# Early products of two output tiles moved into the last rounds of attention, with their loads and banks

## The chip, the cores and the metric

The kernel runs on one core of one Trainium2 chip. The metric is the device time of one execution in microseconds (us), from runs on the chip; the profile comes from one more execution of the same program, which has a time of its own.

## The reference, cut to what matters

x has 2048 rows of 576 numbers in float32. Four layers follow each other: attention, spectral filter, attention, spectral filter, each with a layer norm ahead and a residual behind. Both attention layers use the same weights.

```python
def _A_ref(x, wqkv, wo):                       # 32 heads of 18, window of 256
    q, k, v = split(x @ wqkv)                  # by heads
    scores = einsum("bhqd,bhkd->bhqk", q, k) * Dh ** -0.5
    p = softmax(where(0 <= i_q - i_k < 256, scores, -1e9))
    return heads_joined(einsum("bhqk,bhkd->bhqd", p, v)) @ wo
def _B_ref(x, w_r, w_i):
    return irfft2(rfft2(x) * (w_r + 1j * w_i))

x = x + _A_ref(_layernorm(x), A_wqkv, A_wo)
x = x + _B_ref(_layernorm(x), B_w_r, B_w_i)
x = x + _A_ref(_layernorm(x), A_wqkv, A_wo)
x = x + _B_ref(_layernorm(x), B_w_r, B_w_i)
```

## The kernel before, in words

Every factor of a product is split into a high and a low part of twelve bits of mantissa, so that a product of float32 is two or three products of the faster form (float32r); the parts are named h and l.

**Attention in rounds.** `layer_a` works on 8 groups of 4 heads (n), each with 16 blocks of 128 rows: NX = 128 units x. A loop over t runs from -10 to 129. Round t does the scores of unit t + 10 (LEAD = 10; matmul `S` on TensorE, row maximum with mask on VectorE, L879 to L882), the exponentials of unit t (matmul `E` on TensorE, `P` on ScalarE, masks on GpSimd, L907 to L914), and the product with v of unit t - 2 (`pv`, matmuls `U`, L927). A round handles heads in two pairs: `E` of a pair, `S` of the pair, and after the first pair `pv`. Up to round 102 the products of the q and k projection (`pj`) are spread behind the second pair. Round 117 is the last with scores; from round 118 on a round has only `E` and `U`. After every fourth unit ScalarE copies `U` out (`us`), and `norm` (L934 to L947) transposes it (`tpo`), divides, and stores the rows to DRAM: columns 0 to 447 of the attention's result to o_d, 448 to 575 to o7_d (both stores have line 947). `m_rows` (L884) turns the row maxima round (`tpm`) and sends them with two small DMAs into a row of the q stack.

**Banks.** PSUM has tiles of one bank. `bank` (L840) hands them out in the order of the list `banks`: three with tag S and two with tag E, and from round 103 also the two `pj` ones in front, which leave the list again at round OB + 5 = 125 (OB = NX - 8 = 120). U has a bank of its own. A bank is written again only when the engine that read it has finished.

**The output projection** is done in 16 output tiles u of 128 rows by the class `Out`. The work for a tile: load its rows from o_d (`load`, which also loads the rows of x), split the last 64 columns on GpSimd (`tail`), transpose on TensorE and split on ScalarE or VectorE (`turn`: four transposes, a copy for the high part, a subtraction for the low part), eleven steps of two products each with the first 448 columns (`early`, 22 matmuls `ops` of L578), the transposed last 128 columns (`turn_last`, `split_last`), three more steps (`late`), the sum with x on VectorE (L600), and the sums for the next layer norm (`sums`). `o7` holds the last 128 columns of all tiles; it is filled by the loads `last`, and its last 32 rows directly from the four transposes `tpz` (L1047). Before, ten loads of weights are issued in rounds 105 to 114, the loads of tiles 0 to 2 in 120 to 122, the constants of the next layer (`consts`, six DMAs) in 123, the turns of tiles 0 to 2 in 125 to 127, and all of `early` comes after the last round. DMAs named here are issued by SyncE (SP), in the order of the program: an issue that waits holds all behind it.

**After the rounds** the order is (L1042 to L1071): four steps of tile 0, the `tpz` transposes, the rest of tile 0, tile 1, `turn_last` and `split_last` of tiles 0 to 2, tile 2, `turn(3)`, then `late` of tiles 0, 1, 2 and `turn(4)`. The spectral layer then starts with the products of tile 3 in banks of a new pool.

The time of a round is set by the order in which the program lists work for each engine (no planner reorders it) and by the waits for banks and data.

## Time and profile before

| | us |
|---|---|
| median of 3 runs (1444.2 to 1447.67) | 1447.11 |
| the profiled execution's own time | 1444.81 |
| its span, first to last instruction | 1443.1 |
| TensorE matmul busy in it | 1358.7 (94%) |
| VectorE busy | 947.2 (66%) |
| ScalarE busy | 807.9 (56%) |
| GpSimd busy | 704.5 (49%) |

The mean granted TensorE clock is 0.982 of full speed. PE is the TensorE matmul, PEld its weight loads, DVE VectorE, ACT ScalarE, POOL GpSimd, SP SyncE. A row of the timeline gives the start, the time from the first start to the last end of a run of like instructions (which may overlap the next row's), the engine, the line of the kernel, the tile written and the tiles read, the shapes and the count; in brackets the idle time of the engine before it and what ended that. A product of float32 (`U`, transposes by `ident`) and one of float32r (`E`, `S`, `pj`, `ops`) are both shown as f32; a `U` product counts twice, so that x16 is one `pv`. Matmuls overlap: the distance from start to start is what a matmul costs PE, not its duration.

### The profile page before, as it was taken

Reading aid. Unit: us, or ns where it says so; the run is one execution under the profiler, and the core shown is the slowest. Engines: PE = TensorE matmul, PEld = TensorE weight load, DVE = VectorE, ACT = ScalarE, POOL = GpSimd, SP = SyncE. Lnnn points to the kernel's source line nnn. Section 1 sums busy time; section 2 is a strip of 40 time slices with the busy share of each in tenths; the row PEclk is TensorE's granted clock in tenths of the full one; section 3 lists DMA queues with packets and bytes.
Section 4 is the critical chain, followed back from the end, with each engine's and each line's share of the span. In section 5 each row is a group of like instructions: output and inputs, shape, how many; then the busy total and the mean of one; then the engine's idle time right before and its main releaser. Section 6 shows DMA issues by size and latency. Waiting matters only on the chain. (4 is left out here: it accounts for less than half of the span.)

```text
span 1443.1 us, 35833 instructions
## 1 busy us (share of the span) xinstructions
PE 1358.7 (94%) x12536; PEld 1060.7 (74%) x12536; DVE 947.2 (66%) x3055; ACT 807.9 (56%) x1905; POOL 704.5 (49%) x1203
## 2 busy tenths in 40 slices
PE   7999999999999999987979999999999999999878
PEld 7987666666665889846979876666666658898468
DVE  5348777887777465564543487777877865655645
ACT  5623676666768344425645236766677683443255
POOL 3346566666655343253612565655565553332535
PEclk9999999999999999998989999999999999999989
DMA  7866555545546657676675565555444565576766
GB/s 233 266 193 225 161 165 179 173 151 175 164 142 171 187 179 222 212 235 226 210 238 121 181 223 160 162 155 156 139 145 155 154 172 176 180 222 211 237 221 207
DMA packets 198661, 269.93 MB, mean 187 GB/s; under 512 B 87042, under 2 KB 109154, under 8 KB 197266
## 3 DMA queue, kind: packets, MB, share of 16 engines
q1 hardware_dynamic: 187872, 250.06, 56.1%
q10 hardware_dynamic: 10098, 14.35, 3.2%
q0 software_dynamic: 512, 3.23, 0.8%
q8 instruction: 101, 1.65, 0.5%
q14 instruction: 78, 0.64, 0.1%
HBM read 166.30 MB, written 103.79 MB: 187 GB/s over the span
## 5 line engine op out<-in xcount | busy, mean ns | idle before, releaser
L881 DVE CUSTOM_DVE_ANT_0 jk<-S,mask 128x384 bf16<-128x384 f32 (+2 forms) x1024 | 497.4, 529 | 89.8 <-PE S L879 85.2
L908 ACT ACTIVATE P<-E 128x384 f32<-128x384 f32 (+2 forms) x1024 | 422.5, 477 | 166.2 <-PE E L907 135.9
L910 POOL TENSOR_SCALAR_AFFINE_SELECT P<-P 128x512 f32<-128x512 f32 x256 | 162.4, 634 | 268.1 <-ACT P L908 250.0
L879 PE MATMUL S<-ks,qs 63*128 63x384 f32 (+2 forms) x1024 | 238.9, 364 | 4.3 <-DMA qs<-qk_d 1.0
L907 PE MATMUL E<-qs,ks 64*128 64x384 f32 (+2 forms) x1024 | 220.3, 393 | 2.9 <-DVE sg L823 0.7
L927 PE MATMUL U<-P,vq 128*19 128x128 f32 (+1 forms) x3840 | 202.8, 329 | 2.5 <-POOL P L913 2.0
L907 PEld LDWEIGHTS E<-qs,ks 64*128 64x128 f32 x1024 | 118.5, 183 | 78.1 <-issue 28.5
L879 PEld LDWEIGHTS S<-ks,qs 63*128 63x128 f32 x1024 | 132.7, 184 | 52.2 <-ACT P L908 23.5
L811 PE MATMUL pj<-xh,wqh 64*128 64x512 f32 (+1 forms) x640 | 165.5, 402 | 2.1 <-ACT vt L770 1.7
L927 PEld LDWEIGHTS U<-P,vq 128*19 128x19 f32 x3840 | 90.0, 98 | 95.2 <-issue 34.3
L913 POOL TENSOR_SCALAR_AFFINE_SELECT P<-P 128x512 f32<-128x512 f32 x224 | 142.1, 634 | 0.0
L811 PE MATMUL pj<-xl,wqh 64*128 64x512 f32 (+1 forms) x512 | 127.8, 392 | 0.0
L811 PE MATMUL pj<-xh,wql 64*128 64x512 f32 (+1 forms) x640 | 121.6, 392 | 0.0
L578 PE MATMUL ops<-oroom 128*128 128x288 f32 x784 | 115.2, 304 | 4.4 <-DVE oroom L561 3.0
L578 PEld LDWEIGHTS ops<-oroom 128*128 128x128 f32 x784 | 108.0, 194 | 6.2 <-DVE oroom L561 4.0
L811 PEld LDWEIGHTS pj<-xh,wqh 64*128 64x128 f32 (+1 forms) x640 | 87.7, 186 | 7.3 <-ACT vt L770 2.1
L186 POOL TENSOR_TENSOR eo<-xn 128x287 f32<-128x287 f32 x32 | 26.1, 816 | 126.6 <-ACT xn L184 121.6
L881 DVE DVE_READ_ACCUMULATOR2_ANT m<- 128x1 f32 x1024 | 85.3, 83 | 0.0
L811 PEld LDWEIGHTS pj<-xh,wql 64*128 64x128 f32 (+1 forms) x640 | 73.4, 186 | 7.3
L825 POOL TENSOR_TENSOR sg<-sg 128x512 fp32r<-128x512 f32 x56 | 72.2, 1289 | 4.7
L766 PE MATMUL vps<-wvh,xh 128*128 128x288 f32 x320 | 73.4, 312 | 0.9 <-ACT xh L500 0.9
L811 PEld LDWEIGHTS pj<-xl,wqh 64*128 64x128 f32 (+1 forms) x512 | 71.3, 186 | 3.7
(231 smaller groups left out, 2457.4 us busy)
## 6 DMA issues: line engine op xcount, KB each, us to landing
qk_d<-sg SPq DMA_DIRECT2D x56, 512.0 KB
qs<-qk_d SPq DMA_DIRECT2D x384, 72.0 KB
ks<-qk_d SPq DMA_DIRECT2D x384, 72.0 KB
v_d<-vt SPq DMA_DIRECT2D x32, 304.0 KB
vq<-v_d SPq DMA_DIRECT2D x16, 608.0 KB
wt<-in_w SPq DMA_DIRECT2D x16, 580.0 KB
x<-ofree SPq DMA_DIRECT2D x32, 288.0 KB
ofree<-x SPq DMA_DIRECT2D x16, 576.0 KB
```

The source lines that it names most:

```text
L186: P.tensor_add(eo[:, 0, 1:288], xn[:, 1:288], xn[:, 575:288:-1])
L578: self.nc.tensor.matmul(self.ps[u][n][:, 0:288], x, self.w[p][:, wk * D + n * 288:wk * D + n * 288 + 288], start=first and i == 0, stop=la ...
L766: T.matmul(ps[:, n, 0:288], xT(xk, c), w[:, wk, n * 288:(n + 1) * 288], start=i == 0, stop=i == len(ks) - 1)
L811: T.matmul(ps, w[r, wk], xT(xk, cs)[r], start=s == 0, stop=s == len(ks) - 1)
L825: (P if halves else V).tensor_sub(sg[:, 1], su, sg[:, 0].bitcast(F32))
L879: T.matmul(ps[:, 0:N], q[b:b + 63, pair, i * 128:i * 128 + 128], k[b:b + 63, pair, lo:hi], start=True, stop=True)
L881: V.tensor_tensor_reduce(out=jk[:, 0:N], in0=ps[:, 0:N], in1=mask[:, 384 - N:384], scale=1.0, scalar=-3e38, op0=ALU.add, op1=ALU.max, accu ...
L907: T.matmul(ps[:, 0:nq], k[b:b + 64, pair, j * 128:j * 128 + 128], q[b:b + 64, pair, j * 128:j * 128 + nq], start=True, stop=True)
L908: A.activation(p[:, hl_, 0:nq], ps[:, 0:nq], AF.Exp, scale=SC)
L910: P.affine_select(out=p[:, :, 0:128], in_=p[:, :, 0:128], pattern=[[0, 4], [1, 128]], compare_op=ALU.is_ge, fill=0.0, base=0, channel_mult ...
L913: P.affine_select(out=p[:, :, 256:384], in_=p[:, :, 256:384], pattern=[[0, 4], [-1, 128]], compare_op=ALU.is_gt, fill=0.0, base=0, channel ...
L927: T.matmul(U[32 * h:32 * h + 19, (q0 % 4) * 128:(q0 % 4) * 128 + 128 * (q1 - q0)], vts[n][:, j, h], pt[n, j][:, h, (q0 - j) * 128:(q1 - j) ...
```

## The change

Four products (two steps of two halves) a round of the early products of tiles 0 and 1 are put behind the second pair, in rounds 115 to 125 (`begun`); with them the main columns (0 to 383) of these two tiles are loaded in rounds 111 and 112 and turned in 114 and 118, and their 64-column tails and x follow in 116 and 117 and are turned together in 121 (`turn_tails`). The weights come in the order in which the steps want them, the constants one a round in 115 to 120, the last columns in three loads of 32 partitions. The two `pj` banks leave the rotation at round 113 and hold tile 0's sums; from round 118 two S banks hold tile 1's sums, and the exponentials go round in E, E and the third S bank (F), which later holds half of tile 2. After the rounds, tile 2's early products stand around `tpz` (four transposes each as `turn_z`), one half after the other, then `turn(3)`, `turn_last` and `split_last` of tiles 0 to 2, and the `late` steps as before.

```diff
@@ -506,7 +506,7 @@
     def __init__(self, nc, ident, eps, bp, ov, o7v, srcv, dstv, wo_d, dc_d, gc_d):
         self.__dict__.update(nc=nc, ident=ident, eps=eps, bp=bp, ov=ov, o7v=o7v, srcv=srcv, dstv=dstv, wo_d=wo_d, dc_d=dc_d, gc_d=gc_d)
-        self.ps = {}
+        self.ps, self.dcs = {}, []
     def room(self):
         self.rh = rh = self.bp.tile([128, 5 * S], F32R, tag="xh", name="oroom")
@@ -526,20 +526,24 @@
         self.o7 = f[:, 4736:6784].rearrange("p (n e) -> p n e", n=NT)
     def weights(self, k):
-        c = slice(k // 2 * D, k // 2 * D + D)
-        self.nc.sync.dma_start(self.w["hl"[k % 2]][:, c].bitcast(F32), self.wo_d[k % 2, :, c].bitcast(F32))
-
-    def consts(self):
-
-        self.dcs = []
-        for k, t in enumerate(("wraw", "wraw", "wqh", "wqh", "wql")):
-            d = self.bp.tile([128, 2, NF], F32R, tag=t, name=f"dc{k}", bufs=2)
+        p, b = ("h0", "h1", "h2", "l0", "l1", "l2", "h4", "l4", "h3", "l3")[k]
+        c = slice(int(b) * D, int(b) * D + D)
+        self.nc.sync.dma_start(self.w[p][:, c].bitcast(F32), self.wo_d["hl".index(p), :, c].bitcast(F32))
+
+    def consts(self, k):
+
+        if k < 5:
+            d = self.bp.tile([128, 2, NF], F32R, tag=("wraw", "wraw", "wqh", "wqh", "wql")[k], name=f"dc{k}", bufs=2)
             self.nc.sync.dma_start(d.bitcast(F32), self.dc_d[:, 2 * k:2 * k + 2].bitcast(F32))
             self.dcs.append(d)
-        self.nc.sync.dma_start(self.gc.rearrange("p a c -> p (a c)").bitcast(F32), self.gc_d.bitcast(F32))
-
-    def load(self, u):
-        self.nc.sync.dma_start(self.o[u % 3], self.ov[:, u])
+        else:
+            self.nc.sync.dma_start(self.gc.rearrange("p a c -> p (a c)").bitcast(F32), self.gc_d.bitcast(F32))
+
+    def load_main(self, u):
+        self.nc.sync.dma_start(self.o[u % 3][:, 0:384], self.ov[:, u, 0:384])
+
+    def load(self, u, c=slice(0, 448)):
+        self.nc.sync.dma_start(self.o[u % 3][:, c], self.ov[:, u, c])
         self.nc.sync.dma_start(self.x[u % 5], self.srcv[:, u])
     def last(self, r, c):
@@ -563,6 +567,20 @@
         if last is not None:
             self.split_last(u, last)
+    def turn_main(self, u, tp, copy):
+
+        T, o, oT = self.nc.tensor, self.o[u % 3], self.oT[u % 3]
+        for kt in range(3):
+            T.transpose(tp[:, kt * 128:kt * 128 + 128], o[:, kt * 128:kt * 128 + 128], self.ident)
+        copy(oT[:, 0:384], tp[:, 0:384])
+        self.nc.vector.tensor_sub(oT[:, 512:896], tp[:, 0:384], oT[:, 0:384].bitcast(F32))
+
+    def turn_tails(self, tp):
+        for u in range(2):
+            self.nc.tensor.transpose(tp[:, 128 * u:128 * u + 128], self.tl[u], self.ident)
+        self.nc.vector.tensor_copy(self.rh[:, 5760:7552].rearrange("p (k c) -> p k c", k=2)[:, :, 384:512],
+                                   tp[:, 0:256].rearrange("p (k c) -> p k c", k=2))
+
     def turn_last(self, u, tp):
         self.nc.tensor.transpose(tp, self.o7[:, u], self.ident)
@@ -572,13 +590,13 @@
         self.nc.scalar.copy(oL[:, 0:128], tp)
         self.nc.vector.tensor_sub(oL[:, 128:256], tp, oL[:, 0:128].bitcast(F32))
-    def steps(self, u, ks, first, last):
+    def steps(self, u, ks, first, last, halves=(0, 1)):
         for i, (x, p, wk) in enumerate(ks):
-            for n in range(2):
+            for n in halves:
                 self.nc.tensor.matmul(self.ps[u][n][:, 0:288], x, self.w[p][:, wk * D + n * 288:wk * D + n * 288 + 288],
                                       start=first and i == 0, stop=last and i == len(ks) - 1)
-    def early(self, u, ps, some=slice(0, 11)):
+    def early(self, u, ps, some=slice(0, 11), halves=(0, 1)):
         oT = self.oT[u % 3]
         c = lambda k: oT[:, 128 * k:128 * k + 128]
         if ps:
@@ -589,7 +607,7 @@
         for k in range(3):
             ks += [(c(k), "l", k)]
         ks += [(c(3), "h", 4), (c(3), "l", 4)]
-        self.steps(u, ks[some], some.start == 0, False)
+        self.steps(u, ks[some], some.start == 0, False, halves)
     def late(self, u):
         oL = self.oL[u % 3]
@@ -831,7 +849,7 @@
                             rest()
                 return [lambda s=s, k=k: mm(s, k) for s, k in enumerate(ks)]
-            banks, later, stores = ["S", "S", "E", "E", "S"], [], []
+            banks, later, stores, fixed = ["S", "S", "E", "E", "S"], [], [], []
             def store():
                 while stores:
@@ -842,6 +860,8 @@
                 tag = "S"
                 if t >= 0:
                     banks.append(tag := banks.pop(0))
+                if tag == "F":
+                    return fixed[0]
                 return pp.tile([128, 512], F32, name=name, tag=tag, bufs=3 if tag == "S" else 2)
             vts = {}
@@ -970,6 +990,8 @@
                     goal[t] = 84 + 14 * m - (-14 * (t + 1 - a) // (b - a))
             OB = NX - 8
+            begun = {OB - 5: [(0, 0, 2)], OB - 4: [(0, 2, 4)], OB - 3: [(0, 4, 6)], OB - 2: [(0, 6, 8)], OB - 1: [(0, 8, 9), (1, 0, 1)], OB: [(1, 1, 3)],
+                     OB + 1: [(1, 3, 5)], OB + 2: [(1, 5, 7)], OB + 3: [(0, 9, 11)], OB + 4: [(1, 7, 9)], OB + 5: [(1, 9, 11)]}
             out = Out(nc, ident, eps, bp, ov, o7v, srcv, dstv, wos, dc_d, gc_d)
             for t in range(-LEAD, NX + 2):
@@ -984,8 +1006,11 @@
                 if t == max(goal) + 1:
                     banks[:0] = ["pj", "pj"]
-                if t == OB + 5:
+                if t == OB - 7:
                     banks = [tag for tag in banks if tag != "pj"]
+                if t == NX - LEAD:
+                    first, fixed = [[pp.tile([128, 512], F32, tag="S", name=f"{k}_{n}", bufs=3) for n in range(z)] for k, z in (("ops1", 2), ("F", 1))]
+                    banks = ["E", "E", "F"]
                 want = goal.get(t, len(pj))
                 more, done = pj[done:want], want
                 for pair in range(2):
@@ -1003,6 +1028,9 @@
                         for f in more[:(len(more) + 1) // 2]:
                             f()
                         more = more[(len(more) + 1) // 2:]
+                    if pair == 1 and t in begun:
+                        for u, a, b in begun[t]:
+                            out.early(u, None, slice(a, b))
                 for f in more:
                     f()
                 if copy and t >= 32 and t % 4 == 0 and t < 32 + 16 * len(copy):
@@ -1021,44 +1049,65 @@
                     out.room()
                 if t in range(OB - 15, OB - 5):
                     out.weights(t - OB + 15)
-                if t - OB in (0, 1, 2):
-                    out.load(t - OB)
-                if t == OB + 3:
-                    out.consts()
+                if t - OB in (-9, -8):
+                    out.load_main(t - OB + 9)
+                if t - OB in (-4, -3):
+                    out.load(t - OB + 4, slice(384, 448))
+                if t == OB - 6:
+                    out.turn_main(0, pp.tile([128, 512], F32, tag="pj", name="tpm0", bufs=2), A.copy)
+                    out.ps[0] = [pp.tile([128, 512], F32, tag="pj", name=f"ops0_{n}", bufs=2) for n in range(2)]
+                if t == NX - LEAD:
+                    out.ps[1] = first
+                    out.turn_main(1, bank("tpm1"), V.tensor_copy)
+                if t - OB in (-1, 0):
+                    out.tail(t - OB + 1)
+                if t == OB + 1:
+                    out.turn_tails(bank("tpt"))
+                if t - OB in (0, 2, 3):
+                    out.load((2, 0, 3, 4)[t - OB])
+                if t in range(OB - 5, OB + 1):
+                    out.consts(t - OB + 5)
+                if t == OB + 1:
                     out.last(slice(96, 128), slice(0, 56))
-                if t == NX - 1:
-                    out.last(slice(0, 96), slice(0, 128))
-
-                if t - OB - 3 in (0, 1, 2, 4):
-                    out.tail(min(t - OB - 3, 3))
-                if t - OB - 5 in (0, 1, 2):
-                    u = t - OB - 5
-                    out.turn(u, pp.tile([128, 512], F32, tag="pj", name=f"tpa{u}", bufs=2), V)
-                    if u < 2:
-                        out.load(u + 3)
+                if t - OB in (1, 5, 7):
+                    c = (t - OB) // 3
+                    out.last(slice(32 * c, 32 * c + 32), slice(0, 128))
+
+                if t - OB in (4, 6):
+                    out.tail(2 + (t - OB) // 5)
+                if t == OB + 6:
+                    out.turn(2, bank("tpa2"), V)
                 if t == NX:
                     A.activation(wp.tile([128, 1], F32, name="se", bufs=1), eps, AF.Sqrt)
-            out.early(0, [pp.tile([128, 512], F32, tag="S", name=f"ops0_{n}", bufs=3) for n in range(2)], slice(0, 4))
-
-            for k in range(4):
-                tp = pp.tile([128, 512], F32, tag="E" if k in (1, 2) else "pj", name=f"tpz{k}", bufs=2)[0:32]
+            out.early(2, [fixed[0], None], slice(0, 8), (0,))
+
+            def turn_z(k, tp):
+
                 for a in range(4):
-                    T.transpose(tp[:, 128 * a:128 * a + 128], us[NQ - 1, 3][:, 4 * k + a:512:16], ident)
-                tv = tp.rearrange("p (a h e) -> p a h e", a=4, h=4)
+                    T.transpose(tp[0:32, 128 * a:128 * a + 128], us[NQ - 1, 3][:, 4 * k + a:512:16], ident)
+                tv = tp[0:32].rearrange("p (a h e) -> p a h e", a=4, h=4)
                 rc = wp.tile([128, 4, 4, 1], F32, tag="rc", name=f"rcz{k}", bufs=2)[0:32]
                 V.reciprocal(rc, tv[:, :, :, 18:19])
                 V.tensor_mul(out.o7[96:128, 4 * k:4 * k + 4, 56:128].rearrange("p a (h e) -> p a h e", e=18), tv[:, :, :, 0:18],
                              rc.to_broadcast([32, 4, 4, 18]))
-            out.early(0, None, slice(4, 11))
-            out.early(1, [pp.tile([128, 512], F32, tag=k, name=f"ops1_{k}", bufs=b) for k, b in (("S", 3), ("E", 2))])
-            tp = pp.tile([128, 512], F32, tag="pj", name="tpl", bufs=2)
+
+            def bank_e(name):
+                return pp.tile([128, 512], F32, tag="E", name=name, bufs=2)
+
+            turn_z(0, bank_e("tpz0"))
+            turn_z(1, bank_e("tpz1"))
+            turn_z(2, U)
+            out.early(2, None, slice(8, 11), (0,))
+            turn_z(3, bank_e("tpz3"))
+            out.ps[2][1] = bank_e("ops2_1")
+            out.early(2, None, slice(0, 11), (1,))
+            out.turn(3, U, A)
+            out.tail(4)
+            tp = bank_e("tpl")
             for f in (out.turn_last, out.split_last):
                 for u in range(3):
                     f(u, tp[:, 128 * u:128 * u + 128])
-            out.early(2, [pp.tile([128, 512], F32, tag=k, name=f"ops2_{k}", bufs=2) for k in ("E", "pj")])
-            out.turn(3, U, A)
-            out.tail(4)
             for u in range(3):
                 out.late(u)
                 if u == 0:
@@ -1068,7 +1117,7 @@
                 if u == 1:
                     out.turn_last(4, tp[:, 0:128])
                     out.split_last(4, tp[:, 0:128])
-            out.turn(4, pp.tile([128, 512], F32, tag="E", name="tpa4", bufs=2), A)
+            out.turn(4, pp.tile([128, 512], F32, tag="S", name="tpa4", bufs=3), A)
         spectral(dst, out.dcs, out.gc, ident, out.rh, out.rl, out)
         ctx2.close()
```

## Rows read from the trace of the kernel before

**Rows 1.** The page, busy time of each engine, share of the span and instructions:
```profile
PE 1358.7 (94%) x12536; PEld 1060.7 (74%) x12536; DVE 947.2 (66%) x3055; ACT 807.9 (56%) x1905; POOL 704.5 (49%) x1203
```
**Rows 2.** Chain of waits, 1100 to 1260 us: start, us, engine, tile, line, count:
```profile
1187.45 3.16 ACT P L908 x8
...
1193.71 6.23 DMA o_d<-o
1200.00 5.21 DMA ofree<-o_d
1205.26 0.55 PE tpl L567 x3
...
1214.94 5.50 PE ops L578 x28
1221.09 3.71 PE ops L578 x28
```
**Rows 3.** Timeline of PE, rounds with scores, one with and one without projection:
```profile
1123.39 0.85 PE L927 MATMUL U<-P,vq 128*19 128x256 f32 x16
...
1124.63 0.40 PE L811 MATMUL pj<-xl,wqh 64*128 64x512 f32 x2
...
1125.56 0.35 PE L907 MATMUL E<-qs,ks 64*128 64x384 f32 x2
...
1126.01 0.84 PE L927 MATMUL U<-P,vq 128*19 128x256 f32 x16
...
1170.88 0.85 PE L927 MATMUL U<-P,vq 128*19 128x256 f32 x16
...
1173.05 0.85 PE L927 MATMUL U<-P,vq 128*19 128x256 f32 x16
```
**Rows 4.** Busy time by stretch (us, then PE, PEld, DVE, ACT, POOL, PEclk, DMA, GB/s):
```profile
1164.00:1166.00 2.00, 1.99 (x25) 1.12 (x25) 2.00 (x9) 1.10 (x3) 0.64 (x1) 1.00 1.00 322
```
**Rows 5.** Timeline of PE, rounds without scores:
```profile
1176.46 0.35 PE L907 MATMUL E<-qs,ks 64*128 64x384 f32 x2
...
1184.08 0.85 PE L927 MATMUL U<-P,vq 128*19 128x256 f32 x16 [1.00 <-POOL P L913]
...
1185.22 0.66 PE L937 MATMUL tpo<-ident,us 128*128 128x128 f32 x4
...
1186.19 0.85 PE L927 MATMUL U<-P,vq 128*19 128x256 f32 x16
...
1187.51 0.85 PE L927 MATMUL U<-P,vq 128*19 128x256 f32 x16
...
1190.57 0.39 PE L907 MATMUL E<-qs,ks 64*128 64x256 f32 x2
```
**Rows 6.** Timeline of all engines, the tail after the last round:
```profile
1196.56 1.32 PE L578 MATMUL ops<-oroom 128*128 128x288 f32 x8
...
1197.72 1.91 PE L1047 MATMUL tpz<-ident,us 128*32 128x128 f32 x16
...
1199.39 2.09 PE L578 MATMUL ops<-oroom 128*128 128x288 f32 x14
...
1201.32 0.29 PE L578 MATMUL ops_S<-oroom 128*128 128x288 f32 x1
...
1206.47 0.27 ACT L572 CAST oroom<-tpl 128x128 fp32r<-128x128 f32 x1 [0.36 <-DVE oroom L573]
...
1209.20 0.59 ACT L560 CAST oroom<-U 128x512 fp32r<-128x512 f32 x1 [1.84 <-PE U L556]
...
1209.82 0.56 DVE L561 TENSOR_TENSOR oroom<-U,oroom 128x384 fp32r<-128x384 f32 x1 [2.14 <-ACT oroom L560]
...
1210.29 0.81 DVE L600 TENSOR_TENSOR ofree<-ofree,ops 128x288 f32<-128x288 f32 x2
```
**Rows 7.** Timeline of SP, the DMA issues of the constants:
```profile
1188.15 2.34 SPq L537 DMA_DIRECT2D dc<-dcr  x5
```
**Rows 8.** Busy time by stretch, columns as in rows 4, after the tail:
```profile
1215.50:1216.00 0.50, 0.50 (x4) 0.50 (x4) 0.00 (x0) 0.50 (x1) 0.00 (x0) 0.50 0.77 175
```

## The prediction

> **What bounds the kernel now.** I read the page first: TensorE (PE) is busy for 94% of the span [rows 1], so work that only changes its place gains nothing unless it lands where PE now stands idle. Then the chain of waits, around the end of the second attention: it runs through ScalarE's exponentials, a store to o_d of 6.23 us, the load that waits for it, 5.21 us, and only then to the transposes `tpl` at 1205.26 [rows 2]. There PE waits for a DMA, not for arithmetic. Third, PE's timeline, which shows three regimes. With scores, one group `U` stands 2.17 us after the last (1170.88 to 1173.05, [rows 3]), and in such a stretch VectorE is busy throughout [rows 4]: it sets the pace. Without scores (from the first `E` of round 118 at 1176.46) two groups `U` can stand 1.32 us apart, yet the eight rounds up to the first `E` of round 126 at 1190.57 take 14.11 us [rows 5]. ScalarE sets that pace: eight exponentials in 3.16 us are 1.58 us a round [rows 2], and PE, which runs ahead, waits 1.00 us once [rows 5]. In the tail, from 1196.56 (the first product `ops`) to 1210.29 (the first sum into x), 13.73 us, nearly all is PE [rows 6]. The first attention layer is the same program on another input, so every sum, made here for the second, counts twice.
>
> **What leaves the tail.** Of the 66 early products of tiles 0 to 2, 44 leave. The new tail on PE, from the first product on: 8 products 1.16 us (the distance to `tpz`); 12 of the 16 transposes `tpz`, which take 1.67 us to the next `ops`, 1.25; 3 products at 0.138 (14 in 1.93) 0.41; the other 4 transposes 0.42; 11 products 1.52; 4 transposes of `turn(3)`, 0.42 [rows 6]. That is 5.2 us. The copy of `turn(3)` starts 0.3 later and takes ScalarE 0.59, VectorE's subtraction behind it takes 0.56, and three splits follow at 0.63 us each (ScalarE's half 0.27, and 0.36 in which it waits for VectorE's half before) [rows 6]: 8.5 us to VectorE's first sum into x. Before, the 22 products of tile 2 lay beside the splits; now nothing does. So the tail is 13.73 - 8.5 = **5.2 us shorter** a layer. From that sum on the order stays, and the products at 1214.94 move with it.
>
> **Does the DMA chain let it?** The store of 6.23 us [rows 2] stands behind five loads of constants (297 kB each: 128 x 2 x 290 numbers) that SP issued from 1188.15 [rows 7]. They go to rounds 115 to 120, one a round, and the last load shrinks from 96 partitions to 32 (262 kB). Bounds for the store: 6.23, nothing gained; or its 147 kB at the pace of the 786 kB load, 151 kB/us, 1.0. The store has the smaller rows and some traffic still ahead, but not 1.5 MB; I take 2.5. The load at that pace is 1.7, which I double for its fixed part. The store is issued 2.85 us ahead of the tail, so the data land about 3.5 us into it; PE asks for them at 5.2. The wait for the DMA goes, and what is late next is the splits. On SP's queue six issues of constants, two of main columns and four of tails and x move ahead by 3 to 11 rounds, and tiles 2 to 4 by up to three; at 0.47 us each (2.34 for five, [rows 7]) that is at most 1.4 us in rounds of 1.6 and more. They pass the small DMAs that carry the row maxima, which are wanted four rounds after their issue; I cost them at nothing, and if that cover fails, exponentials wait for as long as the maxima are late. The order of the weights costs nothing either: ten issues before, ten after, in the same rounds.
>
> **What the rounds pay.** In each of eleven rounds (115 to 125) four products stand behind the second pair. Their own time is 4 x 0.138 = 0.55 us. To change from one kind of matmul to another costs PE too: the round with the four transposes `tpo` between its pairs of `E` is 2.11 us from `U` to `U` (1184.08 to 1186.19), the next, without, 1.32 [rows 5]; four transposes are 0.42, so the change costs 0.37. No row has `ops` between two `E`. I bound the overhead by 0 and 0.37 and take 0.2, since `U` to `ops` to `tpz` adds little (8 products in 1.16 us, [rows 6]): 0.75 us a round.
> In rounds 118 to 125 PE then needs 8 x 1.32 + 8 x 0.75 = 16.6 us and 1.7 for what else stands in them (`tpm`, two `tpo`, the main transposes of tile 1, two tails, at 0.42 or less each). That is 18.3 against 14.11: 4.15 more, less 0.3 because ScalarE isn't behind any more when round 126 begins, so **3.85** (2.6 without overhead, 5.2 with 0.37).
> In rounds 115 to 117 PE has slack: a round with products of the projection takes 2.62 us (1123.39 to 1126.01), 0.93 of which are these (1124.63 to 1125.56, [rows 3]), so PE's own need is 1.69 of the 2.17. Each round pays 0.75 - 0.48 = 0.27, three pay 0.8. Tile 0's split in round 114 gives VectorE, at its limit there, one more subtraction (0.56, [rows 6]), partly hidden, and from round 113 the two `pj` banks are out of the rotation: 0.5 for both. So **1.3** (0.4 to 2.0).
> The two together, 5.15, are what the tail gives back.
>
> **The sum.** -5.2 + 5.15 = -0.05 us a layer, nothing for two. The profiled execution took 1444.81 us (span 1443.1 and 1.7 around it), 2.3 less than the median of the runs; on it the sum gives 1444.7, on the median **1447.0**. By the ends of the terms, 2.2 gained or 2.0 lost a layer, 1442.7 to 1451.1.
> One more term can move. The 28 products after `turn(4)` take 5.50 us, the next 28 take 3.71 [rows 2]: the granted clock is 0.50 there, 1.2 GHz of the 2.4 [rows 8], after PE had worked in short pieces between waits. The new tail has such pieces too, so I leave the term at 0, with 0.9 us a layer either way.
>
> **The rivals.**
> *A: insertions cost their own time only.* Then the rounds pay 2.6 + 0.4 a layer, 2.2 is gained: 1442.7, and 1441.2 if the low clock shrinks too. For it: products of the projection between scores show no gap [rows 3]. Against it: 0.79 us for four transposes [rows 5].
> The Trainium skill's page "TensorE: Matmul & The Clock Gate" (Part 2, Step-by-step) says that PE pulls a weight load ahead of running matmuls when their row groups don't conflict or the spare weight buffer takes it. By that rule the overhead vanishes and A's time holds; the round with `tpo` speaks against it.
> *B: the smaller rotation of banks becomes the bound (slower).* From round 118 three banks (E, E, F) carry the exponentials where seven did, from 113 five. A bank comes back after its matmul, the exponential and two semaphores, about 1 us. When PE has been at `pv` or an insertion, the next `E` starts late, ScalarE starves, and `pv` waits for GpSimd's selects. For it: PE has waited for GpSimd's `P` already [rows 5]. Against it: with PE at 2.07 us a round ScalarE's 1.58 leaves 0.5 to return banks. At 0.37 us a round in the 16 rounds of both layers it adds 6 us: 1453. It decides from 0.27 us a round (4.3 us).
> *C: the DMA chain stays last.* If the store still takes 6.23 and the load 3.5, `tpl` starts 6.9 us into the tail, 1.7 late a layer: 1450.4. For it: this chain ends last now [rows 2]. Against it: 1.5 MB no longer stand ahead of it.
> That the early products don't run in the rounds at all I rule out: PE takes its work in the order of the program.
>
> **How the numbers follow.** Forecast 0.46, A 0.27, B 0.20, C 0.07. A measurement tells about 0.3% (4.3 us) from no change. Faster: most of A and the forecast's lower end, 0.25. Slower: B, part of C and the upper end, 0.26. No change: 0.49. The range goes from A with the better clock, 1441.2, to nearly B, 1452.8; the forecast's own is 1442.7 to 1451.1.
>
> **What would show it.** Right: groups `U` of rounds 118 to 125 near 2.05 us apart without waits of PE for ScalarE; rounds 118 to 126 near 18 us instead of 14.11; 8.5 us from tile 2's first `ops` to the first sum into x; no DMA before `tpl` in the chain, splits in its place. Wrong: rounds near 1.85 us (A), waits for `P` ahead of `E` (B), a piece `DMA o_d` in the chain (C). A tail less than 4 us shorter, or rounds that grow by under 3 us in all, would refute the sum.

## The result: slower by 0.43%

The changed kernel takes 1451.4 us (median of 7 runs, 1449.89 to 1454.67), the kernel before 1444.2 us (median of 7 runs, 1441.59 to 1447.67). The ratio is 1.0043, 95% interval 1.0029 to 1.0057: 6.2 us slower (the two medians lie 7.2 us apart). The forecast was no change, with a fair chance for either side; of the rivals, B, the smaller rotation of banks, has the direction and about the time. The profiled execution of the changed kernel took 1449.89 us with a span of 1448.2.

The page's row of busy times answers to [rows 1]. TensorE (PE) is busy 6 us longer for the same 12536 products:

```profile
PE 1364.6 (94%) x12536; PEld 1058.8 (73%) x12536; DVE 947.2 (65%) x3055; ACT 813.3 (56%) x1907; POOL 706.2 (49%) x1203
```

The stretch around the second attention's end can be cut at starts that every kernel has on PE's timeline: the group `U` of round 112, those of rounds 118 and 126, the first product `ops` after the rounds, and VectorE's first sum into x. In us, in the second layer:

| kernel | U 112 to U 118 | U 118 to U 126 | U 126 to tail | tail to first sum | all |
|---|---|---|---|---|---|
| before | 12.48 | 14.28 | 5.42 | 13.73 | 45.91 |
| changed | 15.59 | 20.42 | 5.66 | 8.15 | 49.82 |
| difference | +3.11 | +6.14 | +0.24 | -5.58 | +3.91 |

In the first layer the whole is 50.02 against 45.53, 4.5 more. So the tail gave what was forecast (5.58 here and 5.06 in the first layer, against 5.2), and the rounds took 9.5 where 5.15 were forecast.

The chain of waits answers to [rows 2]: start, us, engine, tile, line, count.

```profile
1208.02 1.25 PE F L596 x8
...
1213.56 0.59 ACT oroom L564
...
1214.18 0.56 DVE oroom L565
1214.73 0.21 DVE oroom L591
...
1215.59 0.28 ACT oroom L590
...
1216.10 0.81 DVE ofree L618 x2
...
1220.46 3.99 PE ops L596 x28
```

No DMA stands in it any more. Between the last early `ops` of tile 2 and the first sum there are the copy and the subtraction of `turn(3)` (L564, L565) and then the splits (L590, L591), as predicted. SP's issues of the last store and of the load that waits for it show why the DMA is gone: the store landed within 2.15 us (2.5 were taken, 6.23 before).

```profile
1204.92 0.37 SPq L967 DMA_DIRECT2D o_d<-o  x1
1207.07 0.32 SPq L550 DMA_DIRECT2D ofree<-o_d  x1
```

One thing was given back behind this stretch. The first 28 products of the spectral layer took 3.99 us in place of 5.50 [rows 2], because in this execution the granted clock did not fall there: 1.00 of 2.4 GHz, against 0.50 in [rows 8] (columns: stretch, us, then busy time of PE, PEld, DVE, ACT, POOL, then clock, DMA share, GB/s).

```profile
1220.50:1221.00 0.50, 0.50 (x4) 0.50 (x5) 0.18 (x2) 0.20 (x1) 0.00 (x0) 1.00 0.72 267
```

It is the same in the first layer (3.98 against 5.50). With 1.5 us given back a layer, 3.9 and 4.5 become 2.4 and 3.0, near the 5.1 us by which the two spans differ. This execution is the shortest of the seven; the median is further off.

The rounds with scores, on PE's timeline, answer to [rows 3]. From `U` to `U` the first round with products takes 2.79 us where it was 2.17:

```profile
1174.06 0.85 PE L947 MATMUL U<-P,vq 128*19 128x256 f32 x16
...
1175.58 0.80 PE L596 MATMUL ops<-oroom 128*128 128x288 f32 x4
...
1176.85 0.85 PE L947 MATMUL U<-P,vq 128*19 128x256 f32 x16
```

A round without scores answers to [rows 5]: 2.24 us from `U` to `U`, where the forecast had 2.07 and the kernel before 1.32 to 2.4.

```profile
1187.91 0.85 PE L947 MATMUL U<-P,vq 128*19 128x256 f32 x16
1188.69 0.44 PE L927 MATMUL E<-qs,ks 64*128 64x384 f32 x1
1188.69 0.44 PE L927 MATMUL F<-qs,ks 64*128 64x384 f32 x1
1189.06 0.79 PE L596 MATMUL ops<-oroom 128*128 128x288 f32 x4
1189.78 0.44 PE L927 MATMUL E<-qs,ks 64*128 64x384 f32 x2
1190.15 0.85 PE L947 MATMUL U<-P,vq 128*19 128x256 f32 x16
```

There is no idle time in brackets: read alone, this row says that PE is full, and that the products and their changes of kind cost 0.92 us a round. That was my first theory. What the row can't tell is whether the rounds would shrink without the products.

### The profile page after: what moved, and what is told of

It reads as the page before. It is cut to its first block, busy times and chain, and to the rows that moved or that the text cites. A ratio compares the mean times of both kernels' runs of the same rounds, so it can differ in the third digit from the quotient of the medians.

```text
span 1448.2 us, 35845 instructions
## 1 busy us (share of the span) xinstructions
PE 1364.6 (94%) x12536; PEld 1058.8 (73%) x12536; DVE 947.2 (65%) x3055; ACT 813.3 (56%) x1907; POOL 706.2 (49%) x1203
## 4 chain that ended last, share of the span: by engine, by line
PE 80%; DMA 6%; DVE 5%; ACT 4%; SPq 2%; issue 2%; POOL 1%; ACTq 0%; DVEq 0%; POOLq 0%
PE pj L829 14%; PE U L947 11%; PE E L927 9%; PE S L899 9%; PE vps L784 8%; PE ops L596 8%; PE po L217 4%; PE pf L217 3%; PE pi L400 2%; PE tpo L957 2%; DMA qs<-qk_d 1%; PE pz L237 1%; SPq L878 1%; PE p L317 1%; PE tpi L201 1%
## 5 line engine op out<-in xcount | busy, mean ns | idle before, releaser
L928 ACT ACTIVATE P<-E 128x384 f32<-128x384 f32 (+2 forms) x998 | 416.0, 474 | 176.7 <-PE E L927 139.7
L927 PE MATMUL E<-qs,ks 64*128 64x384 f32 (+2 forms) x998 | 225.4, 396 | 3.4 <-ACT P L928 0.8
L596 PE MATMUL ops<-oroom 128*128 128x288 f32 x868 | 130.6, 301 | 5.6 <-DVE oroom L565 3.0
L596 PEld LDWEIGHTS ops<-oroom 128*128 128x128 f32 x868 | 117.4, 188 | 12.6 <-issue 4.7
```

Of the source, the lines that this page charges most:

```text
L596: self.nc.tensor.matmul(self.ps[u][n][:, 0:288], x, self.w[p][:, wk * D + n * 288:wk * D + n * 288 + 288], start=first and i == 0, stop=la ...
L927: T.matmul(ps[:, 0:nq], k[b:b + 64, pair, j * 128:j * 128 + 128], q[b:b + 64, pair, j * 128:j * 128 + nq], start=True, stop=True)
L928: A.activation(p[:, hl_, 0:nq], ps[:, 0:nq], AF.Exp, scale=SC)
```

## The experiments

**Theory T**: in the rounds PE is full, each insertion costs 0.92 us (0.55 of its own, 0.37 for changes between `E`, which uses 64 rows of the array, and `ops`, which uses 128). **Theory R** (the prediction's rival B): the rotation of five and three banks makes PE wait for ScalarE, with products or without. Both give about 2.2 us a round, so they had to be taken apart. Every ratio is to runs of the kernel before taken beside it on the same chip. The stages of all runs, in us, second layer, cut as above:

| kernel | U 112 to U 118 | U 118 to U 126 | U 126 to tail | tail to first sum | all | ratio (95%) |
|---|---|---|---|---|---|---|
| e1 products behind pv | 17.21 | 25.35 | 5.65 | 8.15 | 56.36 | 1.0140 (1.0123 to 1.0156) |
| e2 no product in rounds | 15.19 | 20.31 | 5.66 | 14.01 | 55.17 | 1.0151 (1.0129 to 1.0173) |
| e3 loads only | 12.48 | 14.27 | 5.43 | 12.66 | 44.84 | 0.9979 (0.9969 to 0.9990) |
| e4 eight every second round | 16.62 | 21.40 | 5.65 | 8.14 | 51.81 | 1.0080 (1.0063 to 1.0097) |
| e5 products from 118 | 14.51 | 21.78 | 5.65 | 8.17 | 50.11 | 1.0057 (1.0037 to 1.0077) |
| e6 five banks from 113, alone | 15.00 | 14.29 | 5.42 | 13.64 | 48.35 | 1.0034 (1.0020 to 1.0049) |
| e7 three banks from 118, alone | 13.53 | 18.52 | 5.42 | 12.68 | 50.15 | 1.0073 (1.0051 to 1.0095) |
| e8 tile 0 alone, five banks | 13.93 | 18.24 | 5.06 | 9.94 | 47.17 | 1.0003 (0.9992 to 1.0014) |
| e9 as e8, behind pv | 13.93 | 19.16 | 5.06 | 9.94 | 48.09 | 1.0015 (1.0001 to 1.0028) |
| e10 loads, six steps behind pv | 13.14 | 16.24 | 5.42 | 11.28 | 46.08 | 1.0011 (0.9998 to 1.0024) |

### No product in the rounds (e2)

```diff
-            begun = {OB - 5: [(0, 0, 2)], ...
+            begun = {}
...
+            out.early(0, None)
+            out.early(1, None)
             out.early(2, [fixed[0], None], slice(0, 8), (0,))
```

> The changed kernel without any product in the rounds: all 44 of tiles 0 and 1 stand after the last round, ahead of those of tile 2. Loads, turns and banks (five from round 113, three from 118) are those of the changed kernel. Theory T: without insertions rounds 118 to 125 fall from 20.4 to about 14.5 us (ScalarE's pace, 14.1 before), the stretch from the U of round 112 to the first E of round 118 from 15.2 to about 13, and the tail grows from 8.15 to about 14 us; ratio to before 1.000 to 1.002. Rival R (banks): rounds stay above 2.0 us, 118 to 125 above 16.5 us, with waits of PE for ScalarE's P; ratio 1.005 or more.

T's forecast is refuted. Without a single product in them, rounds 118 to 126 take 20.31 us (20.42 with 44 products up to round 125), and the rounds with scores 15.19 (15.59). The ratio is 1.0151, since the tail now has the 44 products again (14.01 us) and the rounds gave nothing back. PE's timeline of one such round:

```profile
1195.81 0.84 PE L947 MATMUL U<-P,vq 128*19 128x256 f32 x16
1196.59 0.44 PE L927 MATMUL E<-qs,ks 64*128 64x384 f32 x1
1196.59 0.44 PE L927 MATMUL F<-qs,ks 64*128 64x384 f32 x1
1196.87 0.34 PE L927 MATMUL E<-qs,ks 64*128 64x384 f32 x1
1197.61 0.44 PE L927 MATMUL E<-qs,ks 64*128 64x384 f32 x1 [0.41 <-ACT P L928]
1197.97 0.85 PE L947 MATMUL U<-P,vq 128*19 128x256 f32 x16
```

ScalarE's timeline has the exponential that reads the first bank; ScalarE had been idle for 0.53 us before it:

```profile
1197.06 0.49 ACT L928 ACTIVATE P<-E 128x384 f32<-128x384 f32 x1 [0.53 <-PE F L927]
```

The second pair of one round and the first of the next stand side by side: four `E` for three banks. The fourth waits until ScalarE has read the bank of the first, 1.02 us after that one's start (1196.59 to 1197.61), and `U`, behind it on PE, waits too. Four `E` take 1.38 us where four with enough banks take 0.55 (in the round 1186.19 to 1187.51 of [rows 5]: 1.32 less the 0.77 of `U`). 1.38 + 0.78 = 2.16 us a round.

### Three banks, alone (e7)

```diff
+                if tag == "F":
+                    return fixed[0]
...
-                if t == OB + 5:
-                    banks = [tag for tag in banks if tag != "pj"]
+                if t == NX - LEAD:
+                    fixed.append(pp.tile([128, 512], F32, tag="S", name="F", bufs=3))
+                    banks = ["E", "E", "F"]
```

> The kernel before with one edit: from round 118 on the exponentials go round in E, E and one S bank; until 117 there are seven banks as before. Theory R: four E stand next to each other, the fourth waits until ScalarE has emptied the bank of the first, and a round takes 2.16 us instead of the mean 1.6 or so; rounds 118 to 125 20 us instead of 14.3, about 6 us a layer, ratio 1.008. Theory T: no insertions, so rounds stay at ScalarE's pace, ratio under 1.002.

What R says of three banks is confirmed on the kernel before. The same pattern stands there, 2.17 us from `U` to `U` with 0.41 us of waiting before the fourth `E`:

```profile
1191.68 0.85 PE L929 MATMUL U<-P,vq 128*19 128x256 f32 x16
...
1193.47 0.44 PE L909 MATMUL E<-qs,ks 64*128 64x384 f32 x1 [0.41 <-ACT P L910]
1193.85 0.85 PE L929 MATMUL U<-P,vq 128*19 128x256 f32 x16
```

Rounds 118 to 126 cost 4.24 us more (18.52 against 14.28), and 1.05 more come between the `U` of round 117 and that of 118 (2.69 against 1.64). The tail is 1.05 shorter (12.68): with the rounds longer, no DMA is waited for ahead of `tpl`. The ratio is 1.0073, a little under the 1.008 expected.

### Five banks, alone (e6)

```diff
-                if t == OB + 5:
+                if t == OB - 7:
                     banks = [tag for tag in banks if tag != "pj"]
```

> The kernel before with one edit: the two pj banks leave the rotation at round 113 instead of 125. Nothing else of the change is in it. Theory R: rounds 113 to 117 take about 2.5 us instead of 2.17, 1.5 to 2.5 us in all; from 118 on five banks stand against ScalarE's pace and cost little (0 to 1 us). 2 to 3 us a layer, ratio 1.003 to 1.004. Theory T: VectorE sets the pace of these rounds, so 0 to 0.5 us a layer, ratio 1.000.

This one line costs 2.5 us in the rounds with scores (15.00 against 12.48) and nothing from 118 on (14.29). A round with five banks, 2.55 us:

```profile
1175.29 0.85 PE L927 MATMUL U<-P,vq 128*19 128x256 f32 x16
1176.07 0.44 PE L907 MATMUL E<-qs,ks 64*128 64x384 f32 x2
1176.35 0.34 PE L879 MATMUL S<-ks,qs 63*128 63x384 f32 x2
1176.52 0.41 PE L907 MATMUL E<-qs,ks 64*128 64x384 f32 x1
1177.09 0.44 PE L907 MATMUL E<-qs,ks 64*128 64x384 f32 x1 [0.15 <-ACT P L908]
1177.47 0.44 PE L879 MATMUL S<-ks,qs 63*128 63x384 f32 x2
1177.84 0.85 PE L927 MATMUL U<-P,vq 128*19 128x256 f32 x16
```

The fourth `E` starts 1.02 us after the first (1176.07 to 1177.09), and the last scores and `U` stand behind it. The interval of the ratio, 1.0020 to 1.0049, holds the expected 1.003 to 1.004, but the runs spread (1446.52 to 1454.78 us), and the profiled execution is the shortest of the twelve.

### The products elsewhere: behind pv (e1), eight every second round (e4), from 118 only (e5)

```diff
                     if pair == 0 and 0 <= t - 2 < NX:
                         pv(t - 2)
+                    if pair == 0 and t in begun:
+                        for u, a, b in begun[t]:
+                            out.early(u, None, slice(a, b))
...
-                    if pair == 1 and t in begun:
...
```

> The changed kernel with the four products of each round put directly behind the group U of pv instead of behind the second pair; banks, loads and counts are the same. Theory T (in the rounds PE is full, and each insertion between two pairs of E costs 0.92 us: 0.55 of its own and 0.37 for two changes between half-height products E and full-height products): behind U, which is full-height too, one of the changes falls away and the four E of two pairs stand together again (0.55 us for four), so a round takes about 1.95 us instead of 2.25, rounds 118 to 125 about 18 us instead of 20.4, and the whole is some 4 to 5 us faster than the changed kernel, ratio to before about 1.001. Rival R (the three and five banks in rotation starve PE): the number of banks is unchanged and pv plus products now stand in one block of 1.3 us between the pairs, so rounds stay at 2.25 or grow; ratio 1.004 or more.

e1 went the way of R: 1.0140. Behind `U` the products don't lie in the wait of the fourth `E` but beside it: 0.78 (`U`) + 0.72 (`ops`) + 1.39 (four `E`) = 2.89 us from `U` to `U`.

```profile
1197.73 0.85 PE L947 MATMUL U<-P,vq 128*19 128x256 f32 x16
1198.51 0.80 PE L596 MATMUL ops<-oroom 128*128 128x288 f32 x4
1199.23 0.44 PE L927 MATMUL E<-qs,ks 64*128 64x384 f32 x1
...
1200.25 0.44 PE L927 MATMUL E<-qs,ks 64*128 64x384 f32 x1 [0.41 <-ACT P L928]
1200.62 0.85 PE L947 MATMUL U<-P,vq 128*19 128x256 f32 x16
```

This tells what the row of the changed kernel could not: with three banks its place between the pairs makes the insertion nearly free. The rounds cost 2.24 with four products and 2.16 without.

```diff
+            begun = {OB - 5: [(0, 0, 4)], OB - 3: [(0, 4, 8)], OB - 1: [(0, 8, 9), (1, 0, 3)], OB + 1: [(1, 3, 7)],
+                     OB + 3: [(0, 9, 11), (1, 7, 9)], OB + 5: [(1, 9, 11)]}
```

> The changed kernel with eight products behind the second pair of every second round (115, 117, ..., 125; four in the last) instead of four in each: the same 44 products in six insertions instead of eleven. Theory T: five changes of kind fewer at 0.37 us, and rounds without insertion fall back to ScalarE's pace while those with one take about 2.8 us: 1.5 to 2 us a layer less than the changed kernel, ratio about 1.002. Rival O (the products' own time is the cost, not the change of kind): the same sum of PE work, ratio 1.004 as the changed kernel. Rival R (banks): longer insertions starve ScalarE longer, ratio over 1.005.

T's 1.002 fails; the 1.0080 lies where R put it, though not by R's way, a longer starving of ScalarE. In a round with eight products (2.77 us) no `E` waits, since the products fill the time, and in one without any (2.16) none of the wait is filled: 21.40 us for 118 to 126, 1.0 more than with four in each.

```diff
+            begun = {OB - 2: [(0, 0, 3)], OB - 1: [(0, 3, 6)], OB: [(0, 6, 9)], OB + 1: [(1, 0, 3)], OB + 2: [(1, 3, 6)],
+                     OB + 3: [(1, 6, 9)], OB + 4: [(0, 9, 11)], OB + 5: [(1, 9, 11)]}
...
-                if t == OB - 7:
+                if t == OB - 4:
...
-                if t == OB - 6:
+                if t == OB - 3:
```

> The changed kernel, but the two pj banks stay in the rotation until round 116, tile 0 is turned in round 117, and all 44 products stand in rounds 118 to 125 (six a round, four in the last two). Rounds 118 and later still have three banks. Theory R (the smaller rotation sets the rounds: five banks make a round with scores 2.55 us instead of 2.17, three make a round without scores 2.16 with no product in it and 2.25 with four): the stretch from the U of round 112 to that of round 118 falls from 15.6 us to about 12.7, and rounds 118 to 125 grow by 0.27 us in each of the six that carry two products more, since the wait is full by then; about 1.3 us a layer less than the changed kernel, ratio about 1.002. Theory T (each insertion costs 0.92 us of PE, banks nothing): three insertions fewer, 2.8 us a layer less in rounds 115 to 117 but 1.7 more later; nearly the same ratio, and the rounds with scores fall only as far as their insertions. The stretch up to 118 tells: T leaves the 2.7 us that stand there without any insertion.

A miss for both. The rounds with scores fell from 15.59 to 14.51 only, not to 12.7: from the `U` of round 115 on five banks are left, and the three distances up to that of 118 are 2.57, 2.55 and 2.89 us, the last with the turn of tile 0 in it (the two conditions at the end of the diff are the rotation and the turn). Six products instead of four cost the expected 0.27 a round (118 to 126: 21.78). The ratio of 1.0057 can't be told from the changed kernel's.

### Enough banks: tile 0 alone (e8, e9)

```diff
+            begun = {OB - 2: [(0, 0, 2)], OB - 1: [(0, 2, 4)], OB: [(0, 4, 6)], OB + 1: [(0, 6, 8)], OB + 2: [(0, 8, 9)], OB + 3: [(0, 9, 11)]}
...
-                    banks = ["E", "E", "F"]
+                    banks = ["S", "S", "E", "E", "S"]
```

> The changed kernel's loads and constants, but only tile 0's products are put into the rounds: four behind the second pair in 118 to 121, two in 122, four in 123. The pj banks stay in the rotation until 116, and from 118 the exponentials keep five banks (three S, two E); tile 1 comes after the rounds as in the kernel before. Theory R: without the shortage of banks an insertion costs PE its own 0.55 us and a small change of kind; PE's need, about 1.32 + 0.6, is close over ScalarE's 1.58: rounds 118 to 123 near 1.9 us, 1.5 us more in all, the tail 2.9 us (22 products) and the 0.84 us of the DMA wait shorter: 2 us a layer faster than before, ratio about 0.997. Theory T: an insertion costs 0.92 us whatever the banks: rounds of 2.24 us, 3.5 us more in all, so no gain over the loads alone, ratio 0.998 to 1.000.

(The `pj` banks leave the rotation at 116, tile 0 is turned in 117 as in e5, and tile 1 comes after the rounds.) With five banks no `E` waits, yet a round with four products takes 2.25 us:

```profile
1181.69 0.85 PE L947 MATMUL U<-P,vq 128*19 128x256 f32 x16
1182.47 0.44 PE L927 MATMUL E<-qs,ks 64*128 64x384 f32 x2
1182.84 0.80 PE L596 MATMUL ops<-oroom 128*128 128x288 f32 x4
1183.57 0.44 PE L927 MATMUL E<-qs,ks 64*128 64x384 f32 x2
1183.94 0.85 PE L947 MATMUL U<-P,vq 128*19 128x256 f32 x16
```

So what T says of one insertion is right as a price, 0.92 us over 1.32: 0.73 from the first `ops` to the next `E`, and 0.37 for each pair of `E` where two pairs together take 0.55. The two limits are equal by chance: three banks without products 2.16, products with banks to spare 2.25, both together 2.24. Relieving one leaves the other, so neither T nor R alone is the cause of the changed kernel's rounds from 118 on: each is enough for them. Had five banks been free there, the 32 products would have left 118 to 126 at some 19.6 us (an estimate: e8's 18.24, with 0.28 for the two products more in round 122, 0.92 for those in round 124 and 0.05 to 0.35 for those in 125, where e8 waits), against 20.42 with three and 14.28 before. The tail fell by 3.8 us, the rounds rose by 5.4 (1.45 up to 118, 3.96 after it); ratio 1.0003.

e9 puts the same products behind `U`, by the lines of e1:

> The kernel with tile 0 alone in the rounds and five banks from 118, but with the products directly behind the group U of pv instead of behind the second pair. Theory K (two causes, each enough for a round of 2.2 us: three banks without any product 2.16, and with five banks the insertion itself, because each change between half-height E and full-height products costs 0.1 to 0.2 us): behind U one change falls away and four E stand together, 0.55 us, so a round with four products is 0.77 + 0.6 + 0.55 = 1.95 us instead of 2.24; rounds 118 to 126 16.8 us instead of 18.24, ratio 0.997 to 0.999. Theory O (four products cost 0.92 us wherever they stand): 2.24 us a round, ratio 1.000. Theory R (with five banks, too, products between pv and the next E starve ScalarE, as behind pv with three banks, where a round took 2.89): over 2.4 us, ratio 1.002 or more.

```profile
1187.79 0.85 PE L947 MATMUL U<-P,vq 128*19 128x256 f32 x16
1188.57 0.80 PE L596 MATMUL ops<-oroom 128*128 128x288 f32 x4
1189.29 0.62 PE L927 MATMUL E<-qs,ks 64*128 64x384 f32 x4
1189.84 0.85 PE L947 MATMUL U<-P,vq 128*19 128x256 f32 x16
```

The round is 2.05 us: 0.73 for the insertion, 0.19 less than between the pairs, so about half of the 0.37 for the changes of kind did go, though 1.95 were expected. The sum over 118 to 126 missed: 19.16 against an expected 16.8. It is 0.92 above e8's, and the round with the transposes `tpt` alone is longer by as much, with a wait of 0.55 us for GpSimd's tail that e8 doesn't have. (A wait of 0.57 for `P` ahead of a `U` stands in both.) That side of e9 I leave open.

### Loads only (e3), and with six steps (e10)

```diff
...
-                if t == OB + 3:
-                    out.consts()
+                if t in range(OB - 5, OB + 1):
+                    out.consts(t - OB + 5)
+                if t == OB + 1:
                     out.last(slice(96, 128), slice(0, 56))
-                if t == NX - 1:
-                    out.last(slice(0, 96), slice(0, 128))
+                if t - OB in (1, 5, 7):
+                    c = (t - OB) // 3
+                    out.last(slice(32 * c, 32 * c + 32), slice(0, 128))
```

> The kernel before with only two parts of the change: the constants are loaded one a round in rounds 115 to 120, and the last columns in three loads of 32 partitions (rounds 121, 125, 127). Theory T: rounds are as before, the store and the load ahead of tpl land some 4 us sooner, PE's wait of 0.84 us before tpl goes and nothing else takes its place; about 1 us a layer, ratio 0.998 to 0.9995. Rival D (the DMA chain was hidden anyway, or the constants disturb the row maxima's DMAs earlier): no change or a wait of E for qs; ratio 1.000 to 1.002.

Faster than both kernels: 1442.14 against 1444.65 us, ratio 0.9979 (0.9969 to 0.9990). The rounds are untouched, the tail is 1.07 us shorter (12.66; 0.55 shorter in the first layer), and the chain of waits has no DMA left there; PE goes from tile 1 straight to `tpl`:

```profile
1198.18 1.84 PE ops L578 x14
...
1202.96 0.33 PE tpl L567 x3
...
1212.42 6.74 PE ops L578 x28
```

```diff
...
-                if t == OB + 5:
+                if t == NX - LEAD:
                     banks = [tag for tag in banks if tag != "pj"]
...
+                    if pair == 0 and t in range(OB, OB + 6):
+                        out.early(0, None, slice(t - OB, t - OB + 1))
...
+                if t == OB - 2:
+                    out.turn(0, pp.tile([128, 512], F32, tag="pj", name="tpa0", bufs=2), V)
```

> The kernel before with constants and last columns loaded as in the run with loads only, and six steps (12 products) of tile 0 in rounds 120 to 125, two products a round directly behind the group U; tile 0 is loaded in 116 and turned in 118, the pj banks stay in the rotation until 117, five banks from 118. Theory K: PE needs about 0.35 us more in six rounds, of which ScalarE's pace hides most (14.27 us for rounds 118 to 126 become 14.5 to 15.3), and the tail loses 12 products, 1.6 us: 0.6 to 1.4 us a layer better than loads only, ratio to before 0.996 to 0.9975. Theory R: five banks starve ScalarE behind the longer block of pv and products, rounds of 2 us, no gain over loads only, ratio 0.998 to 1.000.

A miss: 1.0011, which can't be told from no change. Two products behind `U` cost 0.46 us, 1.78 from `U` to `U`, of which only 0.28 is their own:

```profile
1180.58 0.84 PE L927 MATMUL U<-P,vq 128*19 128x256 f32 x16
1181.36 0.53 PE L578 MATMUL ops<-oroom 128*128 128x288 f32 x2
1181.82 0.62 PE L907 MATMUL E<-qs,ks 64*128 64x384 f32 x4
1182.36 0.85 PE L927 MATMUL U<-P,vq 128*19 128x256 f32 x16
```

Rounds 118 to 126 rose by 1.97 against e3 and those before by 0.66, while the tail fell by 1.38. Six insertions at 0.46 are 2.8 us, so ScalarE's pace hid about 0.8 of them, not most.

## Why the prediction was wrong, point by point

**The tail**: right. 5.58 us less against 5.2 (5.06 in the first layer). The transposes `tpl` start 5.41 us after the first product (1213.36 against 1207.95; 5.2 predicted), the first sum 8.15 (8.5 predicted).

**The DMA chain**: right. No DMA ahead of `tpl`; the store landed within 2.15 us. e3 alone shows what it is worth, 1.07 us of tail in the second layer and 0.55 in the first, and that the earlier constants disturb nothing.

**The rounds with scores**: a failing step. I gave the loss of the two `pj` banks and the split of tile 0 together 0.5 us; the split's 0.56, partly hidden, fills that, so the banks were put at nothing, without a row for it. The banks alone cost 2.5 (e6). The rotation was no spare: with seven banks the fourth `E` of a group finds one, with five it waits for ScalarE. The products, forecast at 0.8, cost 0.4 there (15.59 against 15.19 in e2).

**The rounds without scores**: a failing step, with the largest miss (6.14 against 3.85), in two terms, either of which alone makes such a round 2.2 us long. The first is the banks. "With PE at 2.07 us a round ScalarE's 1.58 leaves 0.5 to return banks" held a mean pace against a mean pace. But the four `E` of two rounds stand together, so the first bank must come back within that group: it does after 1.02 us, and the group takes 1.38 instead of 0.55. Three banks alone cost 4.24 us of 118 to 126 (e7). e2, which has the main transposes and the tails besides (and a wait of 0.42 for a tail's load), stands 1.79 over e7; the 32 products that lie in these rounds add 0.1.

**The change of kind**: the second term. I took 0.2 where the nearest row, `tpo` between `E`, had 0.37; e8 measures 0.37. With banks to spare it brings the same round, 2.25 us. By the estimate behind e8 about 1.5 of the 2.3 us by which these rounds exceed the forecast would have come without any shortage of banks; only the rest, some 0.8, needs the three banks as well. The Trainium skill's "TensorE: Matmul & The Clock Gate" (Part 2, Step-by-step) says that weight loads are pulled ahead of running matmuls when row groups don't conflict or they go to the spare buffer; by that rule rival A's time would hold. The 0.37 us that e8 measures beyond the products' own time, and the 0.18 of e9, speak against a free change in these sequences; that it is the loads that cost it, no run shows.

**Rival B** named one mechanism and the time in which a bank comes back (about 1 us), but was given 0.20, because I looked for the shortage between `pv` and the next `E`, where it isn't. Its sign, waits for `P` ahead of `E`, does not stand in the changed kernel's rounds 119 to 125, since the products fill them; it took e2 to see it. That B's 6 us are so near the measured 6.2 is in part luck: B priced only the rounds without scores, at 0.37 over the forecast's round, where they came out 2.29 us over in eight, 0.29 a round; the rounds with scores added 1.8 a layer that B did not have, and in the profiled execution the clock gave 1.5 a layer back. It is luck, too, that 1451.4 lies inside the stated range: the range stood on 1447.11 for the kernel before, which measured 1444.2 here.

**The clock**: outside its bound of 0.9 us a layer. In the profiled execution the low stretch went away in both layers and gave 1.5 back each. In the traces of all five kernels with the changed tail (this one, e1, e2, e4, e5) the 28 products take 3.98 to 4.00 us in both layers; with other tails anything from 3.98 to 6.74 occurs, and both ends in the two layers of e3's one execution. What decides it stays open.

**Sums of the prediction** that are off, none of which decides: without overhead the rounds from 118 on come to 2.3, not 2.6, if the 0.3 is taken off as it was from the other two values; a store of 2.5 and a load of 3.5 issued 2.85 ahead land 3.2 us into the tail, not 3.5; A's 1441.2 rests on no term, as the bound of 0.9 a layer would give 1440.9.

With the measured terms the sum closes: 3.11 + 6.14 + 0.24 - 5.58 = 3.91 in one layer, 4.5 in the other, 3.0 given back by the clock, 5.4 in all, against 5.1 between the two spans.

## What to carry to other kernels

When work borrows buffers from a rotation, count the rotation against the longest group of requests that stand together in program order, not against the mean pace: three banks for a group of four made a round of 1.32 us one of 2.16, without any borrowed work. A row without idle time shows one limit, not that it is the only one; leave the added work out and see whether the rounds shrink, then relieve the other limit and look again. And split a change into its parts: of those run here, the order of the loads alone was the only one that gained.

## What the runs showed of the hardware that was not expected

Alternating products of 64 and of 128 rows costs TensorE time even when nothing waits: two pairs of `E` side by side take 0.55 us (e9), apart 0.37 each, and four `ops` between them 0.73 instead of 0.55 (e8). `E` and `S`, of 64 and 63 rows, follow each other at 0.28 and 0.17 us (e6), without such a cost. That the rows are what matters, and not the type or the columns, is not shown. A wait and a change of kind that each make a round of 2.2 us do not add up when the inserted work lies in the wait (2.24).
